# The second feed forward's element work in another queue order: Q, the older step's quotient, numerator, logarithm, high part, low part, evictions

## The chip, the cores and the metric

The kernel runs on one core of one Trainium2 chip. The metric is the device time in microseconds, from runs of the whole program; the median of three runs counts. A core has a matrix engine (TensorE; PE in the profile, PEld for its weight loads), a vector engine (VectorE, DVE), an activation engine (ScalarE, ACT), GpSimd (POOL) and SyncE (SP), which here issues most DMAs. Each works through its own queue in order and waits at an instruction for whatever that instruction needs.

## The reference

Attention over 4 x 8 heads with local and strided masks gives x of 2304 tokens by 512. Two feed forwards follow, each 512 to 2048 to 512. The change is in the second:

```python
h = x @ w_in
h2 = h * h
h3 = h2 * h
P = a[0] + a[1] * h + a[2] * h2 + a[3] * h3
Q = 1.0 + np.abs(b[0]) * np.abs(h) + np.abs(b[1]) * h2
g = P / (Q + 1e-06)
out = g @ w_out
```

## The kernel before

The attention and the first feed forward run interleaved over blocks of tokens; the second feed forward comes last, in six blocks of 384 tokens. A block has 16 steps, one for each 128 of the 2048 hidden values. Every float product is made of three matmuls on high and low parts, so each step g of the second feed forward gives TensorE twelve matmuls of 384 columns (`l1`, L409, which fill one bank h) and nine of 512 columns (`l2`, L428, which add to three banks y). The h banks carry the names h and a in turn, two of each, four in all. There are four y banks, and a block takes three: at a block's end the next block's first y group finds one bank free and must wait for the others to be copied out.

TensorE's queue order is l1(g), then l2(g-3): the constant LAG is 3. In between, the other engines make g from h ("element work"), spread over two steps:

- `ew_a` (L456 to L461): ScalarE makes Square (into q), Abs (into z) and Identity (into t) of h; VectorE adds up Q in q (L459), multiplies t by h (L460) and completes the numerator without its constant in h itself (L461).
- `ew_r` (L466 to L468): ScalarE takes the logarithm of q and the exponential of its negative, so that r is about 1/Q; GpSimd multiplies z = q * r.
- `ew_b` (L471, L472), one step later: VectorE improves the quotient, r = (2 - z) * r, and makes h = (h + a0) * r.
- `ew_c` (L477): ScalarE copies h to gh, the high part; `ew_d` (L482): VectorE makes gl = h - gh, the low part. Only with both can l2 run.

The queue order is that in which `run_steps` emits these. For a step g with the older step g-1 in `prev` it is: `second` (which emits l2(g-3) and, after a block's last, marks its y banks for eviction); ew_b of g-1; evictions, if marked; ew_a of g; ew_c of g-1; ew_r of g; ew_d of g-1. `evac` copies bank 0 and 2 of a block on ScalarE (L444) and bank 1 on VectorE (L442), and SP sends them out. Ahead of all this, "early" work of the step is emitted: in four steps of a block an x split for the next block (`x2_split`: xh on ScalarE, L542, xl on GpSimd, L543), and in the first six steps of the second feed forward the last splits of its weights (`w_split`: L163 on ScalarE, L166 on VectorE).

Of the kernel before, what the change touches and what calls it, by code (L numbers as in the profile page):

```python
# [91 lines left out]
def attention_moe_moe_kernel(ctx: ExitStack, tc: tile.TileContext, qk0, qk, vv, w1, w2, consts, a, b, out):  # L92
# [288 lines left out]
    def block(ph, n, xcol, tok):  # L381
        blocks.append(dict(ph=ph, n=n, xcol=xcol, tok=tok, ycol=0, y=None))
        return len(blocks) - 1
# [10 lines left out]
    for n in range(3, 2 * B):  # L394
        bk = block(1, HS, HALF_COL[n], HS * n)
        steps += [(bk, f) for f in range(NF)]
    N1 = len(steps)
    for j in range(NT // NB2):
        bk = block(2, NB2, 0 if j % 2 else RING - NB2, NB2 * j)
# [3 lines left out]
    def l1(bk, f):  # L403
        d = blocks[bk]
        n, cs = d["n"], slice(d["xcol"], d["xcol"] + d["n"])
        h = bank("a" if d["ph"] == 2 and f % 2 else "h")
        ops = [(w, x, c) for c in range(KD) for w, x in ((wh, xh), (wh, xl))] + [(wl, xh, c) for c in range(KD)]
        for k, (w, x, c) in enumerate(ops):
            PE.matmul(h[:, :n], w[d["ph"], f, 0][:, 128 * c:128 * c + 128], x[c][:, cs], start=k == 0, stop=k == len(ops) - 1)  # L409
        return h[:, :n]  # L410
# [19 lines left out]
    def evac(bk):  # L430
        d = blocks[bk]
        n, t0 = d["n"], 0 if bk == bB else d["tok"]
        for c, y in enumerate(d["y"]):
            t = stage("ev")
            if d["ph"] == 2 or bk == bB:
                n = 512
            src = y[:, :n]
            if bk == len(blocks) - 1 and c == len(d["y"]) - 1:
                ACT.activation(out=t[:, :256], in_=src[:, :256], func=AF.Copy)
                DVE.tensor_copy(out=t[:, 256:], in_=src[:, 256:])  # L440
            elif c % 2:
                DVE.tensor_copy(out=t[:, :n], in_=src)  # L442
            else:
                ACT.activation(out=t[:, :n], in_=src, func=AF.Copy)  # L444
            if d["ph"] == 1:
                SP.dma_start(out=x2d[:, c, t0:t0 + n], in_=t[:, :n])
            else:
                (ACT if bk == len(blocks) - 1 and c == len(d["y"]) - 1 else SP).dma_start(out=out[t0 + 128 * c:t0 + 128 * c + 128, :], in_=t)
# [3 lines left out]
    def ew_a(p, bk, h):  # L452
        n = blocks[bk]["n"]
        t = ep.tile([128, NB2], F32, tag="t", name="t")[:, :n]
        q, z, r = (p.tile([128, NB2], F32, tag=k, name=k)[:, :n] for k in "qzr")
        ACT.activation(out=q, in_=h, func=AF.Square, scale=root[:, 0:1])  # L456
        ACT.activation(out=z, in_=h, func=AF.Abs, scale=bab[:, 0:1])
        ACT.activation(out=t, in_=h, func=AF.Identity, scale=ab[:, 3:4], bias=ab[:, 2:3])
        DVE.scalar_tensor_tensor(out=q, in0=q, scalar=1.0 + 1e-6, in1=z, op0=ALU.add, op1=ALU.add)  # L459
        DVE.tensor_tensor(out=t, in0=t, in1=h, op=ALU.mult)  # L460
        DVE.scalar_tensor_tensor(out=h, in0=t, scalar=ab[:, 1:2], in1=h, op0=ALU.add, op1=ALU.mult)  # L461
        return bk, h, q, z, r


    def ew_r(bk, h, q, z, r):
        ACT.activation(out=r, in_=q, func=AF.Ln, scale=LN_SHIFT)  # L466
        ACT.activation(out=r, in_=r, func=AF.Exp, scale=-1.0, bias=biases[:, 1:2])  # L467
        POOL.tensor_tensor(out=z, in0=q, in1=r, op=ALU.mult)  # L468

    def ew_b(bk, h, q, z, r):  # L470
        DVE.scalar_tensor_tensor(out=r, in0=z, scalar=2.0, in1=r, op0=ALU.subtract, op1=ALU.mult, reverse0=True)  # L471
        DVE.scalar_tensor_tensor(out=h, in0=h, scalar=ab[:, 0:1], in1=r, op0=ALU.add, op1=ALU.mult)  # L472

    def ew_c(bk, h):
        n = blocks[bk]["n"]
        gh = gp.tile([128, NB2], F32R, tag="gh", name="gh")[:, :n]
        ACT.activation(out=gh, in_=h, func=AF.Copy)  # L477
        return gh

    def ew_d(bk, h, gh):  # L480
        gl = gp.tile([128, NB2], F32R, tag="gl", name="gl")[:, :blocks[bk]["n"]]
        DVE.tensor_tensor(out=gl, in0=h, in1=gh.bitcast(F32), op=ALU.subtract)  # L482
        return gh, gl


    def ew_new(g, bk, h):
        n = blocks[bk]["n"]
        e = dict(g=g, h=h)
        for k in ("u", "t"):
            e[k] = ep.tile([128, NB2], F32, tag=k, name=k)[:, :n]  # L490
        return e
# [59 lines left out]
    def run(kind, g):  # L551
        for fn, args in plans[kind].get(g, ()):
            fn(*args)
# [82 lines left out]
    def w_abs(g, k):  # L636
        decs.setdefault(g, []).append((k, dec_abs(1, *k)))

    def split1(k, eng):
        d = state.get("dec", ())  # L640
        if k < len(d):
            w_split(d[k][1][1], 1, *d[k][0], eng)

    def order(g):
        return ORD[g] if g in ORD else AB_ORD if g < 2 * NF else C_ORD[g % (2 * NF)] if g % (2 * NF) in C_ORD else REST
# [9 lines left out]
    def run_steps(p, g0, g1):  # L655
        for g in range(g0, g1):
            bk = None
            if g < len(steps):
                bk, f = steps[g]
                h = l1(bk, f)  # L660
            if state["evac"]:
                evac(state["evac"].pop())
            run("early", g)
            if g < N1:
                todo = decs.pop(g, ())
                e = ew_new(g, bk, h)
                fifo = {c: state["e"] + [e] if c in "NMGH" else [e] for c in "UKJVNMGH"}
                state["e"].append(e)
                for c in order(g).translate(COPY if g < 2 * NF else {}):
                    if c.upper() in fifo:  # L670
                        for x in fifo[c.upper()]:
                            if c.upper() not in x and NEED.get(c.upper(), "U") in x | {"U": 1}:
                                x[c.upper()] = True
                                ew_op(c, x)
                                break
                    elif c in "sS":
                        split1(0, POOL if c == "s" else DVE)
                    elif c in "wW":
                        split1(1, POOL if c == "w" else DVE)
                    elif c in "xyzpq":  # L680
                        if c == "x":
                            for _, tm in todo:
                                dec_ops(0, *tm)
                        else:
                            i = "yzpq".index(c)
                            if i % 2 < len(todo):
                                dec_ops(1 + i // 2, *todo[i % 2][1])
                    elif c in "ab":
                        for k in dplan.get(g + 1, ())["ab".index(c):][:1]:
                            w_abs(g + 1, k)  # L690
                    elif c == "T":
                        run("pe1", g)
                        run("pe1e", g)
                    elif c == "L":
                        run("late", g)
                state["e"] = [x for x in state["e"] if "H" not in x]
                state["dec"] = todo
            else:
                for x in state["e"]:
                    for c in "NMGH":  # L700
                        if c not in x:
                            ew_op(c, x)
                state["e"] = []
                second(g, LAG)
                if g == N1:
                    nc.scalar.preload_act_table_set("natural_log_exp_and_others")
                prev = state.pop("prev", None)
                if prev is not None:
                    ew_b(*prev)
                if state["evac"]:  # L710
                    evac(state["evac"].pop())
                if bk is not None:
                    state["prev"] = ew_a(p, bk, h)
                if prev is not None:
                    gh = ew_c(*prev[:2])
                if bk is not None:
                    ew_r(*state["prev"])
                if prev is not None:
                    state["g", g - 1] = ew_d(*prev[:2], gh)
                run("pe1", g)  # L720
                run("pe1e", g)
                run("late", g)
            if g < N1:
                second(g, LAG_AB if bk <= bB else LAG)
            run("pe2", g)
            run("load", g)

    state = {"evac": [], "l2": 0, "e": []}
# [194 lines left out]
```

## Time and profile before

| What | us |
| --- | --- |
| median of 3 runs (972.56 to 974.1) | 972.74 |
| the profiled execution's own time | 970.86 |
| its span, first to last instruction | 969.1 |
| TensorE busy in the span | 917.1 (95%) |
| VectorE busy | 712.1 (73%) |
| ScalarE busy | 690.8 (71%) |
| GpSimd busy | 291.5 (30%) |

The profile is of one execution, and its 1.76 us outside the span are before the first and after the last instruction. Matmuls are pipelined, so TensorE's busy time counts overlaps and short waits as work: whether it waits is better read from the starts of its matmuls. TensorE's granted clock is at full speed (1.00, 2.4 GHz) in every stretch of the second feed forward, from about 542 us to the end.

### The profile page before, as it was taken

The page shows a single profiled execution, that of the slowest core. Times are in us where ns is not written, and L with a number is a line of the kernel's source. Part 1 is how long each engine was busy: PE and PEld are TensorE (multiplying, and loading weights), DVE is VectorE, ACT ScalarE, POOL GpSimd, SP SyncE. Part 2 cuts the span into 40 slices and gives each one's busy share as a digit, 9 for nine tenths or more (in the row PEclk, how much of TensorE's full clock was granted, in tenths as well). Part 3 has the DMA queues.
Part 4 walks back from the last instruction along what each step waited for, and adds up shares of the span by engine and source line. Part 5 has one row for each costly group of instructions (what it writes and reads, how often), then busy time and mean ns, then how long its engine had stood idle before and what let it go on. Part 6 is the DMA issues. An engine that isn't in the chain of part 4 may idle for free.

```text
span 969.1 us, 17280 instructions
## 1 busy us (share of the span) xinstructions
PE 917.1 (95%) x6367; PEld 857.2 (88%) x6367; DVE 712.1 (73%) x1337; ACT 690.8 (71%) x1453; POOL 291.5 (30%) x279
## 2 busy tenths in 40 slices
PE   7578999999999999999999999999999999999997
PEld 6467999989989989999899988898898898898895
DVE  5998745685665676656758788778778787787776
ACT  5987765665674865657658877777777777777875
POOL 2577722132222122221313123232232233232221
PEclk9799999999999999999999999999999999999999
DMA  9766103434324344344236320010100200100000
GB/s 312 265 222 211 45 2 119 163 107 150 113 101 154 104 144 141 131 146 139 93 104 190 120 73 0 12 55 1 58 9 1 66 1 1 66 1 0 33 1 33
DMA packets 51525, 89.35 MB, mean 92 GB/s; under 512 B 4584, under 2 KB 28400, under 8 KB 51440
## 3 DMA queue, kind: packets, MB, share of 16 engines
q1 hardware_dynamic: 50720, 86.58, 27.2%
q10 hardware_dynamic: 720, 1.67, 0.5%
q8 instruction: 50, 0.82, 0.3%
q14 instruction: 35, 0.29, 0.1%
HBM read 70.40 MB, written 17.83 MB: 91 GB/s over the span
## 4 chain that ended last, share of the span: by engine, by line
PE 38%; DVE 22%; ACT 21%; POOL 11%; issue 5%; DMA 2%; POOLq 0%; SPq 0%; ACTq 0%; DVEq 0%
PE h L409 17%; PE y L428 16%; POOL z L468 9%; DVE r L471 7%; ACT r L467 6%; ACT r L466 5%; ACT gh L477 5%; DVE h L472 3%; DVE a L472 3%; PE a L249 2%; DVE dec L157 2%; PE a L364 2%; DMA qk<-in_qk_dram 2%; PE a L345 1%; DVE t L512 1%
## 5 line engine op out<-in xcount | busy, mean ns | idle before, releaser
L409 PE MATMUL h<-xh,w 128*128 128x288 f32 (+3 forms) x1408 | 338.6, 312 | 14.1 <-DVE t L512 11.8
L409 PEld LDWEIGHTS h<-xh,w 128*128 128x128 f32 x1408 | 245.3, 191 | 19.3 <-DVE t L512 13.1
L428 PE MATMUL y<-gh,w 128*128 128x288 f32 (+2 forms) x1024 | 229.1, 300 | 0.6 <-ACT w L163 0.6
L409 PE MATMUL h<-xl,w 128*128 128x288 f32 (+3 forms) x704 | 207.1, 310 | 0.0
L428 PE MATMUL y<-w,gh 128*128 128x512 f32 x576 | 195.9, 393 | 5.5 <-DVE ev L442 4.6
L468 POOL TENSOR_TENSOR z<-q,r 128x384 f32<-128x384 f32 x96 | 97.3, 1013 | 297.9 <-ACT r L467 287.8
L428 PEld LDWEIGHTS y<-gh,w 128*128 128x128 f32 x1024 | 172.0, 189 | 0.8 <-ACT w L163 0.8
L428 PE MATMUL y<-gl,w 128*128 128x288 f32 (+2 forms) x512 | 151.6, 296 | 2.2 <-POOL gl L518 2.1
L409 PEld LDWEIGHTS h<-xl,w 128*128 128x128 f32 x704 | 134.8, 191 | 1.8
L428 PEld LDWEIGHTS y<-w,gh 128*128 128x128 f32 x576 | 108.1, 188 | 28.0 <-DVE ev L442 7.1
L471 DVE SCALAR_TENSOR_TENSOR r<-z,r 128x384 f32<-128x384 f32 x96 | 69.5, 724 | 73.9 <-POOL z L468 73.9
L518 POOL TENSOR_TENSOR gl<-t,gh 128x288 fp32r<-128x288 f32 (+2 forms) x67 | 67.2, 1003 | 184.5 <-ACT gh L516 162.4
L498 ACT ACTIVATE t<-h,biases 128x288 int32<-128x288 f32 (+2 forms) x116 | 57.6, 497 | 89.1 <-PE h L409 78.7
L428 PE MATMUL y<-w,gl 128*128 128x512 f32 x288 | 114.7, 398 | 5.1 <-DVE gl L482 5.0
L508 DVE SCALAR_TENSOR_TENSOR u<-h,t 128x288 f32<-128x288 f32 (+2 forms) x128 | 58.2, 455 | 76.5 <-ACT hs L504 60.8
L409 PE MATMUL a<-xh,w 128*128 128x384 f32 x384 | 106.3, 337 | 0.0
L428 PEld LDWEIGHTS y<-gl,w 128*128 128x128 f32 x512 | 97.0, 189 | 3.0 <-POOL gl L518 2.9
L516 ACT ACTIVATE gh<-t 128x288 fp32r<-128x288 f32 (+2 forms) x128 | 56.6, 442 | 29.3 <-DVE t L512 27.4
L510 ACT ACTIVATE u<-u,biases 128x288 f32<-128x288 f32 (+2 forms) x128 | 67.8, 530 | 12.9 <-DVE u L508 12.6
L409 PEld LDWEIGHTS a<-xh,w 128*128 128x128 f32 x384 | 70.5, 188 | 1.8
L428 PEld LDWEIGHTS y<-w,gl 128*128 128x128 f32 x288 | 54.0, 188 | 20.0 <-DVE gl L482 12.0
L512 DVE TENSOR_TENSOR t<-u,hs 128x288 f32<-128x288 f32 (+1 forms) x91 | 50.5, 555 | 25.6 <-ACT u L510 25.1
(115 smaller groups left out, 1601.1 us busy)
## 6 DMA issues: line engine op xcount, KB each, us to landing
raw<-in_w_dram SPq DMA_DIRECT2D x63, 512.0 KB
qk<-in_qk_dram SPq DMA_DIRECT2D x18, 481.0 KB
wf<-dec SPq DMA_DIRECT2D x32, 256.0 KB
wf<-wf SPq DMA_DIRECT2D x32, 256.0 KB
x2s<-x2d SPq DMA_DIRECT2D x24, 192.0 KB
out_dram<-ev SPq DMA_DIRECT2D x17, 256.0 KB
v<-in_vv_dram SPq DMA_DIRECT2D x16, 240.0 KB
v<-in_vv_dram SPq DMA_DIRECT2D x24, 157.5 KB
```

The lines of the kernel that those rows point to most:

```text
L409: PE.matmul(h[:, :n], w[d["ph"], f, 0][:, 128 * c:128 * c + 128], x[c][:, cs], start=k == 0, stop=k == len(ops) - 1)
L428: PE.matmul(y, l, r, start=first and i == 0 and bk != bB, stop=last and i == 2 and bk != bA)
L467: ACT.activation(out=r, in_=r, func=AF.Exp, scale=-1.0, bias=biases[:, 1:2])
L468: POOL.tensor_tensor(out=z, in0=q, in1=r, op=ALU.mult)
L471: DVE.scalar_tensor_tensor(out=r, in0=z, scalar=2.0, in1=r, op0=ALU.subtract, op1=ALU.mult, reverse0=True)
L472: DVE.scalar_tensor_tensor(out=h, in0=h, scalar=ab[:, 0:1], in1=r, op0=ALU.add, op1=ALU.mult)
L498: ACT.activation(out=k, in_=h, func=AF.Identity, scale=INV_2PI, bias=biases[:, 2:3])
L508: DVE.scalar_tensor_tensor(out=u, in0=h, scalar=INV_2PI, in1=k, op0=ALU.mult, op1=ALU.subtract)
L510: ACT.activation(out=u, in_=u, func=AF.Sin, scale=TWO_PI, bias=biases[:, 3:4])
L512: DVE.tensor_tensor(out=t, in0=u, in1=e.get("hs", h), op=ALU.mult)
L516: ACT.activation(out=e["gh"], in_=t, func=AF.Copy)
L518: (POOL if c == "H" else DVE).tensor_tensor(out=e["gl"], in0=t, in1=e["gh"].bitcast(F32), op=ALU.subtract)
```

## The change

The order in which a step of the second feed forward is emitted. ew_a of step g now comes first and ends at Q (L459); the rest of it, the numerator, is a function of its own, ew_p. The new order is ew_a(g), ew_b(g-1), ew_p(g), ew_r(g), ew_c(g-1), ew_d(g-1), evictions. No instruction is added, removed or changed.

```diff
@@ -457,9 +457,11 @@
         ACT.activation(out=z, in_=h, func=AF.Abs, scale=bab[:, 0:1])
         ACT.activation(out=t, in_=h, func=AF.Identity, scale=ab[:, 3:4], bias=ab[:, 2:3])
         DVE.scalar_tensor_tensor(out=q, in0=q, scalar=1.0 + 1e-6, in1=z, op0=ALU.add, op1=ALU.add)
+        return bk, h, q, z, r, t
+
+    def ew_p(h, t):
         DVE.tensor_tensor(out=t, in0=t, in1=h, op=ALU.mult)
         DVE.scalar_tensor_tensor(out=h, in0=t, scalar=ab[:, 1:2], in1=h, op0=ALU.add, op1=ALU.mult)
-        return bk, h, q, z, r
 
 
     def ew_r(bk, h, q, z, r):
@@ -704,19 +706,19 @@
                 second(g, LAG)
                 if g == N1:
                     nc.scalar.preload_act_table_set("natural_log_exp_and_others")
-                prev = state.pop("prev", None)
+                prev, cur = state.pop("prev", None), None
+                if bk is not None:
+                    cur = state["prev"] = ew_a(p, bk, h)
                 if prev is not None:
-                    ew_b(*prev)
+                    ew_b(*prev[:5])
+                if cur is not None:
+                    ew_p(h, cur[5])
+                    ew_r(*cur[:5])
+                if prev is not None:
+                    gh = ew_c(*prev[:2])
+                    state["g", g - 1] = ew_d(*prev[:2], gh)
                 if state["evac"]:
                     evac(state["evac"].pop())
-                if bk is not None:
-                    state["prev"] = ew_a(p, bk, h)
-                if prev is not None:
-                    gh = ew_c(*prev[:2])
-                if bk is not None:
-                    ew_r(*state["prev"])
-                if prev is not None:
-                    state["g", g - 1] = ew_d(*prev[:2], gh)
                 run("pe1", g)
                 run("pe1e", g)
                 run("late", g)
```

## Rows read from the trace of the kernel before

**Rows 1.** The chain that ended last, whole span, shares by line (the profile's part 4).

```profile
PE h L409 17%; PE y L428 16%; POOL z L468 9%; DVE r L471 7%; ACT r L467 6%; ACT r L466 5%; ACT gh L477 5%; DVE h L472 3%; DVE a L472 3%; PE a L249 2%; DVE dec L157 2%; PE a L364 2%; DMA qk<-in_qk_dram 2%; PE a L345 1%; DVE t L512 1%
```

**Rows 2.** Timeline of TensorE (start us, duration us, what, count, idle time before), second feed forward.

```profile
555.70 0.50 PE L428 MATMUL y<-w,gh 128*128 128x512 f32 x1
...
698.25 0.50 PE L428 MATMUL y<-w,gh 128*128 128x512 f32 x1 [0.64 <-DVE ev L442]
...
699.05 0.33 PE L409 MATMUL h<-xh,w 128*128 128x384 f32 x1
...
905.83 0.34 PE L409 MATMUL h<-xh,w 128*128 128x384 f32 x1
...
951.54 0.33 PE L409 MATMUL a<-xh,w 128*128 128x384 f32 x1
...
964.84 0.39 PE L428 MATMUL y<-w,gh 128*128 128x512 f32 x1
```

**Rows 3.** Waits of weight loads and VectorE from 540 us: total us, times, longest.

```profile
PEld y L428 <- DVE gl L482: 12.0, 20, 1.3
PEld y L428 <- DVE ev L442: 7.1, 6, 1.4
DVE r L471 <- POOL z L468: 73.9, 91, 1.1
```

**Rows 4.** Timeline of VectorE, ScalarE and GpSimd over one step without x split.

```profile
701.04 0.56 DVE L471 SCALAR_TENSOR_TENSOR r<-z,r 128x384 f32<-128x384 f32 x1 [0.81 <-POOL z L468]
...
701.64 0.63 DVE L472 SCALAR_TENSOR_TENSOR h<-h,ab,r 128x384 f32<-128x384 f32 x1
...
702.17 0.55 DVE L459 SCALAR_TENSOR_TENSOR q<-q,z 128x384 f32<-128x384 f32 x1
...
702.30 0.49 ACT L477 ACTIVATE gh<-h 128x384 fp32r<-128x384 f32 x1 [0.93 <-DVE h L472]
...
702.64 0.55 DVE L460 TENSOR_TENSOR t<-t,a 128x384 f32<-128x384 f32 x1
...
702.76 0.53 ACT L466 ACTIVATE r<-q 128x384 f32<-128x384 f32 x1
...
703.22 0.62 DVE L461 SCALAR_TENSOR_TENSOR a<-t,ab,a 128x384 f32<-128x384 f32 x1
...
703.31 0.62 ACT L467 ACTIVATE r<-r,biases 128x384 f32<-128x384 f32 x1
...
703.75 0.55 DVE L482 TENSOR_TENSOR gl<-h,gh 128x384 fp32r<-128x384 f32 x1
...
703.84 0.56 ACT L456 ACTIVATE q<-h,root 128x384 f32<-128x384 f32 x1
...
704.06 1.02 POOL L468 TENSOR_TENSOR z<-q,r 128x384 f32<-128x384 f32 x1 [3.05 <-ACT r L467]
...
704.30 0.57 ACT L457 ACTIVATE z<-h,bab 128x384 f32<-128x384 f32 x1
...
704.76 0.67 ACT L458 ACTIVATE t<-h,ab 128x384 f32<-128x384 f32 x1
```

**Rows 5.** Timeline of ScalarE, GpSimd and VectorE in a step that splits the next x.

```profile
661.00 0.51 ACT L542 ACTIVATE xh<-x2s 128x384 fp32r<-128x384 f32 x1
...
662.20 1.02 POOL L543 TENSOR_TENSOR xl<-x2s,xh 128x384 fp32r<-128x384 f32 x1
...
662.27 1.36 DVE L471 SCALAR_TENSOR_TENSOR r<-z,r 128x384 f32<-128x384 f32 x1 [0.81 <-POOL z L468]
```

**Rows 6.** Timeline of the copies of y at a block boundary.

```profile
695.11 1.07 ACT L444 ACTIVATE ev<-y 128x512 f32<-128x512 f32 x2
...
697.51 0.68 DVE L442 COPY ev<-y 128x512 f32<-128x512 f32 x1
```

**Rows 7.** Timeline of the first boundary: VectorE's weight splits and copies of y.

```profile
549.82 1.69 DVE L166 TENSOR_TENSOR w<-wf,w 128x512 fp32r<-128x512 f32 x2 [0.54 <-ACT w L163]
...
557.59 0.81 DVE L442 COPY ev<-y 128x288 f32<-128x288 f32 x2
```

## The prediction

> **What bounds the kernel now.** The chain that ended last comes first [rows 1]. Over the whole run it stands mostly on TensorE, but 9% of it is POOL's z (L468), 7% each DVE's r (L471), 6% and 5% ACT's Exp and Ln (L467, L466), 5% ACT's gh (L477): the element work of the second feed forward. So I read that part from TensorE's timeline [rows 2]. In its last block, nothing interrupts TensorE from the matmul at 905.83 to that at 951.54: eleven steps of twelve h and nine y matmuls, 4.155 us each (h 2.11, y 2.05). In the three blocks from 699.05 to 905.83 a block of 16 steps takes 68.93 us where 16 x 4.155 is 66.48: 2.45 us are lost per block. From the first y matmul (555.70) to the end of the last (964.84 + 0.39 = 965.23) there are 409.5 us; 92 whole steps and four y groups would need 92 x 4.155 + 4 x 2.05 = 390.5. TensorE could save at most 19 us here.
>
> The waits say on whom [rows 3]: TensorE's weight loads wait 12.0 us in 20 places for gl and 7.1 us in six for DVE's copy of y, once per block boundary. A weight load's wait includes some 0.13 us of its usual spacing, so a boundary costs about 1.05 us (7.1 / 6 - 0.13), the five inside this part 5.3 and the first 1.1. The end, from the last h group's end at 951.54 + 2.11 = 953.65 to 965.23, takes 11.4 us (less 0.2 of modelled drain) for four y groups of 8.2: 3.2. What is left, 19.0 - 6.4 - 3.2 = 9.4, are gl's waits inside the blocks; I count 8.9 of it, since steps that wait for nothing run at up to 4.17.
>
> Why is gl late? One step [rows 4]: z(g) ends on POOL at 705.08; only then can DVE run r(g), h(g) (0.60 + 0.65 us from start to the next engine's start); then ACT copies gh(g) (0.46), and only behind that in ACT's queue come Ln and Exp of step g+1 (0.55, 0.75 to POOL's start), then z(g+1) (1.05 to DVE's start). Sum 4.06 us: a closed ring, so DVE idles 0.81 us a step for z (73.9 us in 91 waits [rows 3]). 4.06 is just under TensorE's 4.155, so whatever adds to the ring stalls TensorE, and it catches up by only 0.09 a step. In the block's four steps that split the next x, POOL's xl runs while DVE wants r, which then takes 1.36 instead of 0.56 [rows 5]: ring 4.87. The element work therefore runs a full TensorE step late almost all the time.
>
> **The change part by part.** No instruction is added or removed; queues alone change. POOL's and SP's order is the same: z(g) per step, and output and x DMAs in the same sequence within the step.
>
> *Ring cut.* DVE now runs q(g), r(g-1), h(g-1), t(g), numerator h(g), gl(g-1); ACT Square, Abs, Identity, Ln, Exp of g, then gh(g-1). Ln(g) needs q(g), which needs only Abs(g), not the older step's h. Take 0 as the start of TensorE's group behind h(g) (the last matmul's modelled end is 0.2 later) and the starts and durations of [rows 4]: Square 0.2, Abs 0.66 to 1.23, Identity to 1.79; q 1.27 to 1.82; Ln 1.85, Exp 2.40 to 3.02; z 3.15 to 4.17. DVE meanwhile r(g-1) 1.80, h(g-1) 2.40 to 3.03, t 2.93, numerator 3.51, gl(g-1) 4.04 to 4.59; gh(g-1) on ACT 3.06 to 3.55, in time for gl. z(g-1) was ready at 0.0, so r never waits. Rings now: DVE's six, 0.53 + 0.60 + 0.53 + 0.58 + 0.53 + 0.50 = 3.3 us; ACT (gh 0.46, Square 0.46, Abs 0.57, q 0.58, Ln 0.55, Exp and wait for h 0.66) 3.3. Either is 0.85 under TensorE's step, so the element work catches up with TensorE and stays there. The wait that is new is Ln on q: behind Ln stand Exp, gh and the copies, and POOL's z and DVE's gl wait for those; it is 0.06 us when ACT is on time (Identity ends 1.79, Ln starts 1.85), since Identity covers q. Buffers don't bind: q, z and r have two each and their last readers (h(g-2) for r) ran in the step before; gh and gl have three, and the y group that read the oldest stands in TensorE's queue before h(g).
>
> *gh and gl* stand later inside a step, behind Ln, Exp, t and the numerator. What is late next would be the y matmuls of step g-1, but TensorE takes them up three steps later: gl(g-1) at 4.59 against a need 4 us on. This slack is the cover; without it the price would be 1.05 us (Ln, Exp) a step.
>
> *x splits* add at most xh's 0.51 on ACT [rows 5]: 3.8, still under 4.155. Their xl on POOL would run 4.17 to 5.2, before the next q at 5.43: clear by 0.25. The Trainium skill, SBUF — State Buffer, "Who interferes with whom", says that DVE instructions with two SBUF inputs and GpSimd instructions reading SBUF lock each other out for a whole instruction; q and r are such a pair, now back to back. The trace agrees (r 1.36 behind xl [rows 5]). So all gl stalls inside the blocks go: -8.9 (bounds 0 and -8.9).
>
> *Evictions* move from before q to the queue's end. What waits for them is the first y group of the next block: its first bank is free, the second needs ACT's copy, the third DVE's. New places: ACT's two copies [rows 6] from 3.5 to 4.1 and 4.6, DVE's from 4.54 to 5.22 (behind gl). TensorE wants the banks 4.84 and 5.53 after its h group's end: margins 0.7 and 0.25. So the five boundaries lose nothing: -5.3. Behind the copies stand Square (0.14 late) and q (in time); on SP the three output DMAs, issued by the copies' ends, and behind them x loads that are split two steps (8 us) later. If the element work stayed late by x us at a boundary, the stall would be x - 0.25. I take x = 0, since the last x split stands six steps before and each step catches up 0.85.
>
> *First boundary.* Here the weight splits (two of 512 on ACT and DVE a step, 1.69 us on DVE with what POOL takes of it [rows 7]) keep the element work late. In the step after the first, DVE can start q when the split ends, at 551.4, r and h to 553.2, gl to 554.7; next step: splits, q at 555.8, Exp to 557.55, gh to 558.05, ACT's copies 558.0 to 558.7, DVE's 559.05 to 559.85 (now 557.59 to 558.40). The y group that began at 555.70 begins at 558.45 and ends near 560.5, against 555.70 + 2.05 + 1.1 = 558.9 now: +1.6 (bounds 0, and 2.75 for the whole delay of the first copy).
>
> *Tail.* The four last y groups lose 3.2 us because r(95) waits on the ring. New, from the last h group's end: gl of step 94 at 4.59 (need 4.33), r(95) 4.55, h 5.15, gh 5.8, gl 6.33 to 6.88 (need 6.7): some 0.6 lost in place of 3.2: -2.6.
>
> Sum: -8.9 - 5.3 + 1.6 - 2.6 = -15.2 us. On the profiled execution: span 969.1 to 953.9, its time 970.86 to 955.7 (1.76 us lie around the span). The median of the runs is 972.74, 1.9 above that execution; less 15.2: **957.5 us**.
>
> **The rivals.** *Evictions only just late*: the margin 0.25 is thin. If DVE's copy waits as it does now (about 1 us per boundary), 5.3 come back: 962.8. For it: six waits on DVE's copy stand in the trace. Against: they arise from a queue that runs a step late.
>
> *Port collisions*: z or xl meets q or r each step: +0.8 on a ring of 3.3 is 4.1, and the x splits stall TensorE as now. The 8.9 stay, the evictions and tail gain half: about 967. Against: by the times above POOL is free when q and r run.
>
> *Slower, evictions late by a queue*: if the element work stays a full step late, DVE's copy comes behind q, t, the numerator and gl instead of before them: 0.53 + 0.47 + 0.58 + 0.53 = 2.1 us later at five boundaries, 10.6, and 1.6 at the first, with nothing gained: 985. It decides from a lateness of about 3.3 us at the boundaries (5 x (3.3 - 0.25) = 15.2); for that the new ring must be 4.1 us or more. The Trainium skill, PSUM — Partial Sum Buffer, "Summary: rules for kernel authors", says to evacuate promptly; taken strictly that is this case. The boundary stalls of [rows 2, 3] agree that a late copy costs TensorE time, but not that order alone makes it late.
>
> *No change*: gh, now behind Exp, closes a ring as long as the old (3.3 plus a wait I don't see, 0.85 or more): the stalls remain, 972.7.
>
> **How the numbers follow.** Forecast (954.5 to 960) 0.70; evictions just late (960 to 964) 0.15; collisions (964 to 970) 0.06; no change 0.04; slower 0.05. Low end: no loss at the first boundary (-1.6) and a little more in the tail, 955.3; high end 963.3, most of the second case. About 0.2% (2 us) is what a measurement can tell from no change: faster 0.91, same 0.04, slower 0.05.
>
> **What would show it.** After: DVE's r no longer waits for POOL (73.9 us now, under 10 then); Square starts within 0.3 us of the h group's end in mid-block; steps are 4.155 in every block; the weight loads' waits on gl and on DVE's copy fall under 2 us each, except a start of the first y group some 2.7 us later; r never takes 1.36. It is wrong if x lateness persists at boundaries, if q shows times near 1.3, or if Ln waits on q for more than about 0.1 us while ACT is late.

## The result

| | median us | runs | ratio to the kernel before (95% interval) |
| --- | --- | --- | --- |
| before | 972.56 | 5 (970.76 to 974.1) | |
| changed | 957.24 | 5 (956.05 to 961.01) | 0.9847 (0.9826 to 0.9868) |

The change saves 1.5%, with 957.5 us forecast and 955.3 to 963.3 given. The profiled execution of the changed kernel took 957.24 us, its span is 955.5. Lines behind L462 have moved by two: Ln and Exp are now L468 and L469, z L470, the quotient L473 and L474, gh L479, gl L484; t and the numerator are L463 and L464.

The chain that ended last, shares of the span by engine and by line, which answers to [rows 1]:

```profile
PE 79%; DVE 9%; ACT 6%; issue 3%; DMA 2%; POOL 1%; SPq 0%; ACTq 0%; DVEq 0%; POOLq 0%
PE y L428 35%; PE h L409 27%; PE a L409 10%; DVE dec L157 2%; PE a L249 2%; PE a L364 2%; PE a L345 1%; DVE t L514 1%; ACT dec L143 1%; DMA v<-in_vv_dram 1%; DVE dec L155 1%; DVE dec L605 1%; ACT u L512 1%; ACT raw L148 1%; DMA raw<-in_w_dram 1%
```

POOL's z, DVE's r and ACT's Exp are no longer among its largest lines: TensorE holds 79% where it held 38%. The waits from 540 us, which answer to [rows 3] (first TensorE's weight loads, then VectorE, then ScalarE):

```profile
PEld y L428 <- ACT ev L444: 3.0, 1, 3.0
PEld y L428 <- DVE gl L484: 1.0, 2, 0.6
...
DVE q L459 <- ACT z L457: 80.4, 92, 2.9
...
ACT q L456 <- PE a L409: 34.2, 40, 1.1
ACT q L456 <- PE h L409: 29.6, 44, 0.9
```

The 20 waits for gl are 2, the six for DVE's copy none; one of 3.0 us for ACT's copy is new. DVE waits for Abs and ACT's Square for TensorE: both now follow the matmuls instead of the other way round. One step of the three engines without an x split, like that of [rows 4]:

```profile
697.40 0.58 ACT L456 ACTIVATE q<-h,root 128x384 f32<-128x384 f32 x1 [0.87 <-PE h L409]
...
697.88 0.57 ACT L457 ACTIVATE z<-h,bab 128x384 f32<-128x384 f32 x1
...
698.48 0.56 DVE L459 SCALAR_TENSOR_TENSOR q<-q,z 128x384 f32<-128x384 f32 x1 [0.91 <-ACT z L457]
...
698.96 0.55 DVE L473 SCALAR_TENSOR_TENSOR r<-z,r 128x384 f32<-128x384 f32 x1
...
699.08 0.53 ACT L468 ACTIVATE r<-q 128x384 f32<-128x384 f32 x1
...
699.63 0.62 ACT L469 ACTIVATE r<-r,biases 128x384 f32<-128x384 f32 x1
...
700.20 0.49 ACT L479 ACTIVATE gh<-a 128x384 fp32r<-128x384 f32 x1
...
700.38 1.01 POOL L470 TENSOR_TENSOR z<-q,r 128x384 f32<-128x384 f32 x1 [3.15 <-ACT r L469]
...
701.19 0.55 DVE L484 TENSOR_TENSOR gl<-a,gh 128x384 fp32r<-128x384 f32 x1
```

TensorE's h group ended just before Square, which waited 0.87 us for it. From Square: Abs 0.48, q 1.08, r 1.56, Ln 1.68, Exp 2.23, gh 2.80, z 2.98, gl 3.79. The prediction's list, counted from Square (its 0.2), says 0.46, 1.07, 1.60, 1.65, 2.20, 2.86, 2.95, 3.84.

TensorE's timeline, which answers to [rows 2]: the first y group (TensorE stood 2.71 us ahead of it), two y groups 90 steps apart, the last h group, the last matmul:

```profile
559.73 0.50 PE L428 MATMUL y<-w,gh 128*128 128x512 f32 x1 [2.71 <-ACT ev L444]
...
564.02 0.40 PE L428 MATMUL y<-w,gh 128*128 128x512 f32 x1
...
938.39 0.39 PE L428 MATMUL y<-w,gh 128*128 128x512 f32 x1
...
940.44 0.33 PE L409 MATMUL a<-xh,w 128*128 128x384 f32 x1
...
951.23 0.39 PE L428 MATMUL y<-w,gh 128*128 128x512 f32 x1
```

From 564.02 to 938.39 there are 90 steps without a stall, 4.160 us each.

| TensorE, us | before | changed | difference | forecast |
| --- | --- | --- | --- | --- |
| first 384-column h group to end of first y group | 542.30 to 558.89: 16.59 | 543.66 to 561.91: 18.25 | +1.7 | +1.6 |
| from there to the start of the last h group | 392.65 | 378.53 | -14.1 | -14.2 |
| from there to the end of the last matmul | 951.54 to 965.23: 13.69 | 940.44 to 951.62: 11.18 | -2.5 | -2.6 |
| second feed forward | 422.93 | 407.96 | -15.0 | -15.2 |

What is left to the span's difference of 13.6 us is the part ahead, which no edit touches and which took 1.4 us more in this execution (543.66 against 542.30).

### The profile page after: what moved, and what is told of

The parts are those of the page before. It is cut to its first block, busy times and chain, and to the rows that moved or that the text cites. A ratio compares the mean times of both kernels' runs of the same rounds, so it can differ in the third digit from the quotient of the medians.

```text
span 955.5 us, 17292 instructions
## 1 busy us (share of the span) xinstructions
PE 913.3 (96%) x6367; PEld 862.2 (90%) x6367; DVE 694.2 (73%) x1337; ACT 699.8 (73%) x1453; POOL 290.8 (30%) x279
## 4 chain that ended last, share of the span: by engine, by line
PE 79%; DVE 9%; ACT 6%; issue 3%; DMA 2%; POOL 1%; SPq 0%; ACTq 0%; DVEq 0%; POOLq 0%
PE y L428 35%; PE h L409 27%; PE a L409 10%; DVE dec L157 2%; PE a L249 2%; PE a L364 2%; PE a L345 1%; DVE t L514 1%; ACT dec L143 1%; DMA v<-in_vv_dram 1%; DVE dec L155 1%; DVE dec L605 1%; ACT u L512 1%; ACT raw L148 1%; DMA raw<-in_w_dram 1%
## 5 line engine op out<-in xcount | busy, mean ns | idle before, releaser
L428 PE MATMUL y<-w,gh 128*128 128x512 f32 x576 | 193.2, 390 | 2.7 <-ACT ev L444 2.7
L470 POOL TENSOR_TENSOR z<-q,r 128x384 f32<-128x384 f32 x96 | 97.4, 1015 | 282.5 <-ACT r L469 272.3
L428 PE MATMUL y<-w,gl 128*128 128x512 f32 x288 | 112.7, 391 | 0.2 <-DVE gl L484 0.2
L459 DVE SCALAR_TENSOR_TENSOR q<-q,z 128x384 f32<-128x384 f32 x96 | 53.7, 560 | 80.4 <-ACT z L457 80.4
L409 PE MATMUL a<-xl,w 128*128 128x384 f32 x192 | 64.9, 338 | 0.0
```

Of the source, the lines that this page charges most:

```text
L428: PE.matmul(y, l, r, start=first and i == 0 and bk != bB, stop=last and i == 2 and bk != bA)
```

## Experiments

Each run stands beside the kernel before on the same chip. The questions: is it the ring (the closed chain of waits and queue orders from one step to the next) that set the pace, and only that; is the place of the evictions a price or a gain; and how much time has the element work now to spare. "Second feed forward" below is the last line of the table: 422.9 us before, 408.0 changed.

**Evictions alone (e1_evict_last).** The old order, evictions last:

```diff
                 if prev is not None:
                     ew_b(*prev)
-                if state["evac"]:
-                    evac(state["evac"].pop())
...
                     state["g", g - 1] = ew_d(*prev[:2], gh)
+                if state["evac"]:
+                    evac(state["evac"].pop())
```

> The old order with one part of the change, the evictions moved to the queue's end. If the time comes from the ring, this part gains nothing: a block lasts as long as its ring (16 x 4.06 + 4 x 0.80 for the x splits = 68.2 us), whether TensorE stands at the boundary or at gl; 968 to 977 us. If late evictions are a price of their own (the slower rival: 2.1 us at five boundaries and 1.6 at the first), 985 us. If moving the evictions is what gained, 958 to 965 us.

Measured 970.7 us, 0.9973 (0.9961 to 0.9986). TensorE's timeline at one boundary (the y group begins at 699.45) and its weight loads' waits from 560 us:

```profile
701.71 0.51 PE L428 MATMUL y<-w,gh 128*128 128x512 f32 x1 [1.41 <-ACT ev L444]
```

```profile
PEld y L428 <- ACT ev L444: 13.9, 6, 4.4
```

The boundary stall grew from 1.05 to some 1.7 us, but no wait for gl is among the 11 largest any more. The y groups at the boundaries begin at 631.00, 699.45, 767.78 and 835.86: 68.3 us a block, the ring's 68.2, where the kernel before takes 68.9. A TensorE that stands longer at the boundary gives the element work time to come nearer, and is not stopped inside the block. The 2.4 us gained fit what DVE's copy (0.6 us of its queue, five times) costs ahead of q and no longer costs at the queue's end, where DVE waits for z anyway: from r to r across a boundary 4.66 us pass before (696.38 to 701.04, with the copy of [rows 6] between) and 4.05 here (698.29 to 702.34). The second feed forward, 419.7 us, is 3.2 shorter; its tail, from the last h group on, takes 11.2 us as in the changed kernel, and its first y group waits 4.05 us for ACT's copy.

**Half the cut: Ln and Exp ahead of gh (e2_log_first).**

```diff
-                if prev is not None:
-                    gh = ew_c(*prev[:2])
                 if bk is not None:
                     ew_r(*state["prev"])
                 if prev is not None:
+                    gh = ew_c(*prev[:2])
                     state["g", g - 1] = ew_d(*prev[:2], gh)
```

> The old order with one part, Ln and Exp ahead of gh on ACT; DVE still runs the older step's quotient ahead of Q. Ring theory: Ln now waits for q, which stands behind r and h of the older step on DVE, so the ring closes through q: r 0.60, h 0.53, q 0.58, Ln 0.55, Exp 0.75, z 1.05 = 4.06 us, as long as before: 970 to 975 us. If it is only gh ahead of Ln that holds the steps together: most of the gain, 957 to 962 us.

Measured 973.36 us, 1.000 (0.9991 to 1.001). The largest new wait from 560 us:

```profile
ACT r L466 <- DVE q L459: 100.3, 93, 1.7
```

ACT no longer waits for h but for q, 1.1 us a step: the ring closes through Q instead of gh, and is as long. From r to r 4.07 us pass, and 4.86 where xl holds r up, both as before.

**The other half: Q first (e3_q_first).** The changed kernel with gh back ahead of Ln:

```diff
                 if cur is not None:
                     ew_p(h, cur[5])
-                    ew_r(*cur[:5])
                 if prev is not None:
                     gh = ew_c(*prev[:2])
+                if cur is not None:
+                    ew_r(*cur[:5])
+                if prev is not None:
                     state["g", g - 1] = ew_d(*prev[:2], gh)
```

> The new order with gh put back ahead of Ln and Exp on ACT; Q still first on DVE. Ring theory: r 0.60, h 0.65, gh 0.46, Ln 0.55, Exp 0.75, z 1.05 = 4.06 us stands again: 969 to 976 us. If it is only Q's place on DVE that counts: 957 to 962 us.

Measured 1005.76 us, 1.0334 (1.0319 to 1.035): neither of the two answers. The chain that ended last, in order of time (start, us, what), through one step without an x split:

```profile
814.94 0.49 ACT gh L479
815.43 0.42 ACT r L468
815.90 0.50 issue
816.40 0.56 ACT q L456
816.96 0.48 ACT z L457
817.47 0.58 DVE q L459
818.05 0.48 DVE r L473
818.53 0.03 issue
818.55 0.64 DVE h L474
819.22 0.49 ACT gh L479
```

I had looked for the old ring, through z, and missed another that needs no z: gh waits for h; Ln and Exp stand behind gh, the next Square and Abs behind Exp; q waits for Abs, r and h stand behind q. It is 4.28 us from gh to gh (814.94 to 819.22), above TensorE's 4.155. The step that splits an x takes 5.25 us (809.69 to 814.94), with xh in ACT's queue and this, from the timeline:

```profile
812.35 1.01 POOL L545 TENSOR_TENSOR xl<-x2s,xh 128x384 fp32r<-128x384 f32 x1
...
812.63 1.15 DVE L459 SCALAR_TENSOR_TENSOR q<-q,z 128x384 f32<-128x384 f32 x1 [1.40 <-ACT z L457]
```

q takes 1.15 us in place of 0.55, behind xl on POOL: the collision of the prediction's second rival. So Q first is by itself a loss, Ln first is worth nothing, and both together give 15 us.

**Numerator ahead of the quotient (e4_numerator_first).** The changed kernel without the new function's purpose:

```diff
                 if bk is not None:
                     cur = state["prev"] = ew_a(p, bk, h)
+                    ew_p(h, cur[5])
                 if prev is not None:
                     ew_b(*prev[:5])
                 if cur is not None:
-                    ew_p(h, cur[5])
                     ew_r(*cur[:5])
```

> The new order, but the numerator (t, then h) stands with Q ahead of the older step's quotient on DVE, as one piece. Ln and Exp still wait for nothing old. Ring theory: a new ring closes through gh: q to t 0.56, t 0.58, h 0.53, r 0.53 to 0.60, older h 0.66, gh 0.46, Square 0.46, Abs 0.57, to q 0.04 = 4.4 us, over TensorE's 4.155, and each x split and eviction on ACT adds to it: about 7 us more per block, 985 to 1000 us, slower than before. If it is enough that Ln waits for nothing old: 957 to 960 us.

Measured 1004.15 us, 1.032 (1.0302 to 1.0339), 4 us past the range's end. gh in two steps, from the timeline:

```profile
807.71 0.49 ACT L479 ACTIVATE gh<-a 128x384 fp32r<-128x384 f32 x1 [1.16 <-DVE a L474]
...
812.11 0.49 ACT L479 ACTIVATE gh<-h 128x384 fp32r<-128x384 f32 x1 [1.16 <-DVE h L474]
```

4.40 us from gh to gh, as worked out. The range was too low since it took 7 us a block; a block takes 74.7 us (y groups at boundaries begin at 708.48 and 783.18), 8.2 more than TensorE's 66.5. That the numerator stands behind the older quotient is thus worth 47 us of the order's time.

**Evictions early at the first boundary (e5_first_evict_early).** Ahead of ew_a, for the block of the first feed forward only:

```diff
+                if state["evac"] and blocks[state["evac"][-1]]["ph"] == 1:
+                    evac(state["evac"].pop())
                 prev, cur = state.pop("prev", None), None
```

> The new order, with the evictions at the first boundary alone put at the head of their step. The profile after shows TensorE idle 2.71 us there, for ACT's copy. If that idle time is the price of the place: 2.5 to 2.9 us less than the changed kernel, 954 to 955 us. If the weight splits around it hold TensorE anyway: 957 us.

Measured 955.73 us, 0.9821 (0.9807 to 0.9834). TensorE's first y group now follows its h group at once (no idle time stands at the row, where the changed kernel has 2.71 us):

```profile
557.96 0.40 PE L428 MATMUL y<-w,gh 128*128 128x512 f32 x1
```

Second feed forward 405.2 us, 2.7 less than changed: the idle time, all of it. The total lies 0.7 us above the range given.

**All evictions early (e6_evict_first, e11_evict_first_again, beside e10_changed_again).** The same without the condition on `ph`.

> The new order, with all evictions at the head of their step, ahead of Square and Q. At the later boundaries ACT then waits some 2.3 us for the y group, which makes that step's element work late by 2 to 2.5 us; gl has 4 us of slack and each step catches up 0.85, so nothing is lost: as the run with the first boundary alone, 954 to 955 us. If the place of the evictions matters once the ring is cut: 2 us lost at each of five boundaries, 963 to 966 us.

> The changed kernel itself, for comparison on the same chip with the next run: 956 to 959 us.

> The new order with all evictions at the head of their step, once more beside the changed kernel: 2.4 to 2.9 us less than that, the whole idle time at the first boundary.

Measured 954.83 us, 0.981 (0.9797 to 0.9823). The comparison on one chip: changed 958.1 us, 0.9842 (0.9829 to 0.9855); all early 955.11 us, 0.9816 (0.9802 to 0.9829). The totals differ by 3.0 us and their intervals still touch; the second feed forward is 408.0 against 405.2 us. At the later boundaries ACT's timeline of the first of these runs:

```profile
686.65 0.60 ACT L444 ACTIVATE ev<-y 128x512 f32<-128x512 f32 x1 [1.50 <-PE y L428]
...
688.01 0.60 ACT L444 ACTIVATE ev<-y 128x512 f32<-128x512 f32 x1 [0.76 <-PE y L428]
...
688.50 0.58 ACT L456 ACTIVATE q<-h,root 128x384 f32<-128x384 f32 x1
...
691.70 0.58 ACT L456 ACTIVATE q<-a,root 128x384 f32<-128x384 f32 x1
...
694.89 0.58 ACT L456 ACTIVATE q<-h,root 128x384 f32<-128x384 f32 x1
...
698.80 0.58 ACT L456 ACTIVATE q<-a,root 128x384 f32<-128x384 f32 x1 [0.61 <-PE a L409]
```

ACT waits 1.50 and 0.76 us for the y group, its Square is late by about 2 us, and the next two come 3.20 and 3.19 us later. That is the new ring, not held back by TensorE: 3.2 us where 3.3 was worked out. In the fourth step Square waits for TensorE again, and no y group of that block is late. So once the element work has time to spare, the evictions may stand at a step's head or at its end; only at the first boundary, where the weight splits use that time up, their place costs 2.7 us.

**Time to spare (e7_one_more, e8_two_more, e9_three_more).** One, two or three useless low parts more on DVE in each step; they write a scratch tile and leave the output as it is:

```diff
+    def ew_x(bk, h, gh):
+        x = ep.tile([128, NB2], F32R, tag="hs", name="extra")[:, :blocks[bk]["n"]]
+        DVE.tensor_tensor(out=x, in0=h, in1=gh.bitcast(F32), op=ALU.subtract)
...
                     state["g", g - 1] = ew_d(*prev[:2], gh)
+                    for _ in range(1):
+                        ew_x(*prev[:2], gh)
```

> The new order with one useless DVE instruction more per step, a second low part behind gl (about 0.5 us; the output is not touched). Ring theory: DVE's six give 3.3 us, with this 3.8, under TensorE's 4.155: within 1 us of the changed kernel, 957 to 958 us. If the element work has no spare time left: 95 x 0.5 = 48 us more.

> The same with two useless DVE instructions more per step. Ring theory: 3.27 + 2 x 0.5 = 4.25 to 4.3 us, now 0.1 to 0.15 above TensorE's 4.155: 2 to 3 us per block, less some 4 us that the lag of three steps takes in: 965 to 972 us, with DVE without idle time. If the spare time is larger than 0.85 us: 957 to 958 us.

> The new order with three useless DVE instructions more per step. With two, the trace puts DVE's ring at 0.47 + 0.59 + 0.53 + 0.58 + 0.53 + 3 x 0.47 = 4.1 us, just under TensorE's 4.155, with nothing lost in mid-block. Ring theory: with three 4.6 us, 0.4 above TensorE's step: 95 x 0.4 less some 4 us of lag, 990 to 1000 us. If TensorE's own step still sets the pace: 960 to 965 us.

Measured 959.83 us (0.9859; 0.9845 to 0.9872), 962.17 us (0.9881; 0.9863 to 0.9898) and 1004.82 us (1.0323; 1.0309 to 1.0337): all three lie outside the ranges given, the first two between the two answers that I had put. Second feed forward: 409.1 and 411.4 us with one and two, 1.1 and 3.4 more than changed. Those microseconds are lost where the element work has no time to spare: at the first boundary (TensorE stands 3.2 and 3.7 us in place of 2.7 for ACT's copy, and with two 0.6 more for DVE's) and at the tail, and with two 0.9 us at the second boundary as well. After that no y group of either run is late in mid-block. With two, DVE rests no more while it catches up, and its ring can be read from q of two steps:

```profile
574.17 0.55 DVE L459 SCALAR_TENSOR_TENSOR q<-q,z 128x384 f32<-128x384 f32 x1
...
578.27 0.55 DVE L459 SCALAR_TENSOR_TENSOR q<-q,z 128x384 f32<-128x384 f32 x1
```

4.10 us, where I had given 4.25 to 4.3. With three, DVE never rests:

```profile
807.23 0.55 DVE L459 SCALAR_TENSOR_TENSOR q<-q,z 128x384 f32<-128x384 f32 x1
...
811.78 0.55 DVE L459 SCALAR_TENSOR_TENSOR q<-q,z 128x384 f32<-128x384 f32 x1
```

4.55 us a step. The knee is between two and three instructions: 4.10 and 4.55 us on either side of TensorE's 4.155. With three I gave 990 to 1000; a block takes 73.5 us (y groups at 708.60 and 782.08), 16 x 4.55 = 72.8 and DVE's copy, and the first block's weight splits on DVE come on top, while I had counted 4 us of lag as free: in the first block that lag is used up already.

## Why the prediction was right

*The ring cut.* Right, and shown by both halves: Ln first alone 1.000, Q first alone 1.033, together 0.985. The ring was given as 3.3 us; run free it measures 3.2. What decides is the ring's time summed over a block, with all that adds to it, against TensorE's 66.5 us. The old ring, in e1 and e2 too, takes 4.06 us and in the four steps with an x split 0.80 more, where xl on POOL holds r up (r takes 1.36 us in 20 steps before [rows 5], in e1 and in e2): 68.2 without DVE's copy, and the element work sets the pace. DVE's ring with two more instructions takes 4.10 and meets no collision: 16 x 4.10 and 0.6 for DVE's copy are 66.2, and TensorE sets the pace from the third block on. So the length of the old ring, so close under TensorE's step, is only a part of the cause: the prediction's "whatever adds to the ring stalls TensorE" is the other. Without the collisions and with DVE's copy the old ring would by this sum take 65.6 us, less than TensorE, and the run with two more instructions, which closes another ring of that length, keeps 11.5 of the 15.0 us. The changed order removed both, and no run has the old ring without the collisions.

*The gl stalls inside the blocks (-8.9) and the five boundaries (-5.3).* Right in sum, -14.1 measured. At the later boundaries DVE's copy ends 0.3 us ahead of need, as reckoned: in one boundary step of the changed kernel (y group from 692.97, so its third bank is wanted at 692.97 + 1.37 = 694.34)

```profile
693.32 0.68 DVE L442 COPY ev<-y 128x512 f32<-128x512 f32 x1
```

it ends at 694.00. But the experiment with all evictions early says that this margin was no condition of the gain: there is room for two microseconds of lateness. My first rival took a thin margin for a risk that it isn't.

*The first boundary (+1.6).* +1.7 measured. The early evictions show that the place itself costs 2.7 us, of which 1.1 was lost at that boundary before as well.

*The tail (-2.6).* -2.5. The size is right; that r(95) waits on the ring is not all of it, since e1 keeps the old ring and its tail takes 11.2 us as well. By e1, what the tail needs is element work that is not late when it begins; no run tests that alone.

*gh and gl later in a step.* Covered, as named: two gl waits are left, 1.0 us together.

*The port.* No collision in the changed kernel. In a step that splits the next x, from the timeline:

```profile
663.91 1.02 POOL L545 TENSOR_TENSOR xl<-x2s,xh 128x384 fp32r<-128x384 f32 x1
...
665.19 0.56 DVE L459 SCALAR_TENSOR_TENSOR q<-q,z 128x384 f32<-128x384 f32 x1 [0.89 <-ACT z L457]
```

xl ends 0.26 us ahead of q, where 0.25 was reckoned, and q and r take 0.56 and 0.55 us. The lock itself stands as the Trainium skill, SBUF — State Buffer, "Who interferes with whom", has it: e3 shows q at 1.15 us behind xl. The page speaks of a cost that this order avoids and that the old order and e3's pay.

*The slower rival.* Its price was wrong. It put 2.1 us on each boundary if the element work stays late; e1, the old order with the evictions last, has late element work and is 0.3% faster than before. With three more instructions the new order has it too: TensorE then loses 5.3 to 6.4 us at a boundary, and a block still lasts its ring's sum, 73.5 us. While the ring sets the pace, a stall moved to another place is paid once, in the block's sum of ring times, and not again at the boundary. With that, "evacuate promptly" (the Trainium skill, PSUM — Partial Sum Buffer, "Summary: rules for kernel authors", which gives the tight space as its reason) has, as a rule on order, no support in e1, and in the changed kernel only at the first boundary, 2.7 us.

What the sum did not foresee is the part ahead, 1.4 us slower in the profiled execution; its time scatters by 3 us over the executions here (the first 384-column matmul between 542.3 and 545.6), so the agreement of the totals to 0.3 us is partly luck, that of the second feed forward to 0.2 us less so.

## What to carry to other kernels

When an engine that should be full stalls for a result, follow the wait once round: if the queue orders of the other engines close a ring over steps, its length, with all that adds to it in some of the steps, against the full engine's time for the same steps decides, and every stall that you see is only where the difference comes out. List all rings of a new order, those through a queue's order alone too (e3's needed no slow operation, just gh ahead of Ln). Here a ring below the pace by a fifth made the place of the evictions cheap, and one just below it let 20 small collisions through to the full engine.

## What was not expected of the hardware

TensorE's granted clock can fall after a stall inside a busy stretch. In the run with three more DVE instructions, TensorE stands at a boundary for ACT's copy (first view, its timeline), and the windows around it (second view: busy times of the engines, then PEclk) show the clock:

```profile
713.10 0.80 PE L428 MATMUL y<-w,gh 128*128 128x512 f32 x1 [3.28 <-ACT ev L444]
713.70 0.63 PE L428 MATMUL y<-w,gl 128*128 128x512 f32 x1
714.12 1.05 PE L428 MATMUL y<-w,gh 128*128 128x512 f32 x2
```

```profile
714.00:716.00 2.00, 2.00 (x6) 1.52 (x6) 2.00 (x6) 1.04 (x3) 0.00 (x0) 0.50 0.31 119
...
718.00:720.00 2.00, 2.00 (x11) 1.68 (x10) 2.00 (x5) 1.58 (x3) 0.41 (x1) 1.00 0.91 297
```

After 3.28 us without a matmul the granted clock is 0.50 (the 1.2 GHz level), and matmuls of 512 columns follow each other in 0.42 us instead of 0.23, before it is back at 1.00. The length of the stall alone does not decide. With two more instructions TensorE stands longer at the first boundary, and the clock stays at 1.00 (the same two views):

```profile
561.32 0.50 PE L428 MATMUL y<-w,gh 128*128 128x512 f32 x1 [3.65 <-ACT ev L444]
```

```profile
561.00:564.00 3.00, 2.30 (x9) 1.60 (x10) 3.00 (x7) 3.00 (x7) 0.64 (x1) 1.00 0.14 49
564.00:570.00 6.00, 6.00 (x33) 5.60 (x32) 5.93 (x13) 3.84 (x8) 1.01 (x1) 1.00 0.87 290
```

In the changed kernel the 2.71 us at the first boundary leave it at 1.00 too. What else decides is not shown here. With three more instructions DVE's ring sets the pace and a block lasts the ring's sum, so the slower matmuls show nowhere in its time.

Independent DVE instructions of 0.55 us each start 0.46 to 0.47 us apart (three extra ones take 1.47 us together), where I had counted 0.5. That is a third of why two fitted; the rest is that DVE's own six take some 3.16 us (4.10 less two of 0.47) and not 3.27.
